# Another count of TensorE's instructions in a kernel's planner, and rows transposed through DRAM and VectorE in place of TensorE

## The chip, the cores and the metric

The kernel runs on one core of one Trainium2 chip. A core has five engines that run side by side, each with its own queue, in order: TensorE (PE; its weight loads are listed as PEld), VectorE (DVE), ScalarE (ACT), GpSimd (POOL) and SyncE (SP), which here issues nearly all DMAs. The metric is the device time in microseconds (us) of one execution. A profiled execution is a run of its own, with a time of its own.

## The reference

Two blocks follow one another, all in float32.

```python
# q, k, v: (4, 8, 768, 48) = batch, heads, steps, head size; beta: (4, 8, 768)
k_n = k / (np.linalg.norm(k, axis=-1, keepdims=True) + 1e-06)
for t in range(S):
    y[:, :, t] = np.einsum('bhd,bhde->bhe', q[:, :, t], state)
    v_old = np.einsum('bhde,bhd->bhe', state, kt)
    state = state + bt[:, :, :, None] * np.einsum('bhd,bhe->bhde', kt, vt - v_old)
x = y.transpose(0, 2, 1, 3).reshape(B * S, H * D)      # 3072 tokens of 384
rms = np.sqrt(np.mean(x * x, axis=-1, keepdims=True) + 1e-06)
xn = x / rms * rms_g
g = xn @ w_gate                                        # 384 x 1536
out = (g * (1.0 / (1.0 + np.exp(-g))) * (xn @ w_val)) @ w_out
```

The first is a recurrence over 768 steps (a delta rule), the second a gated feed-forward layer on its normalized output.

## The kernel before

**Tiling.** The steps are cut into 12 chunks (c = 0 to 11) of 64 steps. A chunk has 4 x 64 = 256 tokens, two tiles of 128. For each chunk there are these parts, each a function:

- `load`: k, q, v from DRAM by DMAs on SP; `norms` (L621): the inverse norms of k.
- `prep` (L812): k scaled and transposed on TensorE (`turn`, L582), scores of k with k (L605), a triangular inverse by 15 double steps on VectorE (L908, L914), for which the matrix is laid out anew through DRAM (dkk, dx, dxt), and a merge on TensorE (L963, L983). The merge uses half of the tile yn as scratch (L972).
- `qpart` (L638): q transposed and scores of q with k (L605). From chunk 2 on, q is brought into SBUF in squares of 32 x 32 by 16 small DMAs, and one VectorE transpose that works on 32 x 32 squares (`square_turn`, L613) does the rest.
- `recur` (L1000): products of k and q with the state (L1022), the inverse times the rest (L1069), and two products whose results are the chunk's output and the change of the state (L1105, L1174). The output rows are put into yn (128 x 2 x 384; L1044 and L1205), their mean square is taken (L1211), the root on GpSimd (L1224), and L1239 scales yn by it. Then yn has to be transposed into xf (128 features x 6 blocks of 128 columns), with the feature gains g_sb put in: six TensorE transposes into PSUM (L1256) and six ScalarE scalings out of it (L1260). Seven sums on VectorE (L1275) make the other eleven blocks of xf that the fast matrix product needs.
- `ffn` (L1403), chunks 2 to 11: 30 products, each four 128 x 128 x 128 matmuls (L1416), with evacuations on ScalarE (L1428) and VectorE (L1426), then the gate (L1432, L1433). `down` (L1454) does seven products of six matmuls each (L1473), with sums before and after (L1465, L1482), and stores. Chunks 0 and 1 go through `ffn_plain` (L1323, L1305).

yn and xf have one buffer each. xf of chunk c can be written only when the last product (L1416) of chunk c-1 has read it; yn is free again when it has been transposed.

**What sets the order.** Nothing is issued as the functions are called. Each call of `P.add` records an operation with its engine, a modelled duration, its dependencies, its PSUM banks and, for TensorE, `size`, its number of instructions (a float32 matmul counts four: two weight loads and two matmuls). `Plan.run` (L225) then makes many rounds: `forward` (L117) is a list scheduler that takes, over all engines, the operation that can start first (ties by a key), `backward` (L197) makes new keys from the latest starts, and these are shaken by random numbers. The round with the earliest modelled end gives the order, and in this order the operations are issued to their engines. The model has a penalty for a change of TensorE's tile shape (STICK) and an account of TensorE's instructions: a backlog that grows by `size` and falls at a fixed rate (FETCH, AHEAD; FETCH0, AHEAD0 before 130 us). A backlog over the store makes an operation's key worse by 2 x STICK, and its end later.

Until 70 us on the model's clock, TensorE is given filler matmuls (L1579) when it would stand idle.

Of the kernel before, what the change touches and what calls it, by code (L numbers as in the profile page):

```python
# [22 lines left out]
STRETCH = {"PE": 1.5, "ACT": 1.5, "DVE": 1.4, "POOL": 1.2, "SP": 1.0}  # L23
ENGINES = ("PE", "ACT", "DVE", "POOL", "SP")
OVERLAP = {"PE": 0.0, "ACT": 0.1, "DVE": 0.08, "POOL": 0.06, "SP": 0.0}
ROUNDS = 150
FETCH, AHEAD = 67.0, 160.0
EARLY, FETCH0, AHEAD0 = 130.0, 42.0, 130.0
STICK = 1.0
EARLYN = ()  # L30
RELEASE = (4.7, 29.5, 32.8, 35.2, 41.3, 40.8, 44)
KSQ, XSQ = 99, 99
DRAIN, REFILL, GRACE = 0.1, 0.2, 0.0
SHAKE = 0.12
SPARE = 1.0
# [22 lines left out]
def fillers(a, b):  # L58

    if a == 0.0:  # L60
        return [4, 4, 1]
    n, t = [], a
    while t < b - SPARE:
        n.append(4 if b - t > 1.5 else 2 if b - t > 0.9 else 1)
        t += 0.22 * n[-1] + 0.02
    return n


class Plan:
# [47 lines left out]
    def forward(self, banks, until):  # L117

        at = dict.fromkeys(ENGINES, 0.0)
        held = {"DVE": 0.0, "POOL": 0.0}  # L120
        cand = {e: [] for e in ENGINES}
        free = list(banks)
        for op in self.ops:
            op.wait, op.at = len(op.deps), op.ready
            for g in op.acquire:
                g.taken, g.uses = False, g.left
            if not op.wait:
                cand[op.eng].append(op)
        order, server, end_, mode = [], 0.0, 0.0, 0
        backlog = 0.0  # L130
        lanes = [0.0] * 8
        while len(order) < len(self.ops):
            best = None
            for e in ENGINES:
                for op in cand[e]:
                    s = max(op.at, at[e])
                    if op.dma:
                        s = max(s, lanes[0])
                    if op.port:
                        s = max(s, held["POOL" if e == "DVE" else "DVE"])  # L140
                    n = sum(not g.taken for g in op.acquire)
                    if n > len(free):
                        continue
                    if n:
                        s = max(s, free[n - 1])
                    key = op.key + (STICK if op.mode is not None and op.mode != mode else 0.0)
                    rate, store = (FETCH, AHEAD) if s > EARLY else (FETCH0, AHEAD0)
                    if op.size and backlog + op.size - rate * op.dur > store:
                        key += 2.0 * STICK
                    seen = max(at["PE"], s - GRACE) if op.mode is not None and op.mode == mode < 128 else s  # L150
                    if best is None or (seen, key, op.n) < best[0]:
                        best = (seen, key, op.n), op, s
            if best is None:
                return None
            _, op, s = best
            cand[op.eng].remove(op)
            for g in op.acquire:
                if not g.taken:
                    g.taken = True
                    free.pop(0)  # L160
            op.start = s
            if op.mode is not None and op.mode != mode:
                s += DRAIN if op.mode < 128 else REFILL
                op.start, mode = s, op.mode
            end = s + op.dur
            if op.eng == "PE":
                if s - at["PE"] > 1.4 and s > until:
                    end += 1.6
                rate, store = (FETCH, AHEAD) if s > EARLY else (FETCH0, AHEAD0)
                fill = 6.0 if s < until else 0.0  # L170
                backlog = max(0.0, backlog - (rate - fill) * (s - at["PE"])) + op.size - rate * op.dur
                late = max(0.0, backlog - store) / rate
                backlog, end = max(0.0, backlog - rate * late), end + late
            at[op.eng] = end - min(OVERLAP[op.eng], op.dur)
            if op.port:
                held[op.eng] = end
            end_ = max(end_, end)
            for g in op.release:
                g.uses -= 1
                if not g.uses:  # L180
                    free.append(end + 0.1)
                    free.sort()
            if op.dma:
                server = max(end + 0.9, server) + op.work
                end = server
                lanes = lanes[1:] + [end + 0.7]
            op.end = end
            for u in op.users:
                u.wait -= 1
                u.at = max(u.at, at[op.eng] if u.eng == op.eng and not op.dma else end + op.hop(u) + u.slack)  # L190
                if not u.wait:
                    cand[u.eng].append(u)
            order.append(op)
        self.end = end_
        return order
# [28 lines left out]

    def run(self, free, filler=None, until=0.0):  # L225
        self.first_priorities()
        best = None
        self.ends = []
        rng = random.Random(47)
        for k in range(ROUNDS):  # L230
            order = self.forward([t for t, _ in free], until if filler else 0.0)
            if order is None:
                break
            self.ends.append(self.end)
            if best is None or self.end < best[0]:
                best = self.end, [(op, op.start) for op in order]
            self.backward()
            for op in self.ops:
                if op.first:
                    op.key = op.n - 2000.0  # L240
                op.key += SHAKE * (k % 3) * rng.uniform(-1.0, 1.0)
        self.end = best[0]
        pe = 0.0
        free = list(free)
        for op, s in best[1]:
            op.start = s
            for g in op.acquire:
                if g.t is None:
                    g.t = free.pop(0)[1]
            if filler and op.eng == "PE":  # L250
                if s < until:
                    filler(fillers(pe, s))
                pe = s + op.dur
            op.fn()
            for g in op.release:
                g.left -= 1
                if not g.left:
                    free.append((s + op.dur + 0.1, g.t))
                    free.sort(key=lambda x: x[0])
# [1355 lines left out]
```

## Time and profile before

| what | us |
|---|---|
| median of 3 runs (698.35 to 700.17) | 698.62 |
| the profiled execution | 695.48 |
| its span, first to last instruction | 693.8 |
| PE: time in which a matmul ran | 679.1 (98%) |
| PEld: time in which weights were loaded | 619.7 (89%) |
| DVE busy | 540.1 (78%) |
| ACT busy | 304.0 (44%) |
| POOL busy | 139.9 (20%) |
| products L1416, both groups, x2400 | 181.6 + 124.6 |
| transposes of yn L1256, x72 | 10.9 |
| transposes of q on VectorE L613, x10 | 12.4 |

How to read the rows of the profile: a group is "line, engine, operation, out<-in, shape, xcount | busy us, mean ns of one | idle time of the engine before them and what ended it". A float32 matmul of the program stands as two rows of MATMUL and two of LDWEIGHTS. Matmuls are pipelined, so a mean of 277 ns is longer than the pitch at which they follow one another. "issue" means that an engine waited for nothing that the profile shows. A queue's name with a q at the end (SPq) is the engine's sequencer. In the list of DMAs the last number is the median time from issue to landing.

### The profile page before, as it was taken

What the parts mean: (1) busy time and instruction counts of PE and PEld (TensorE: products, weight loads), DVE (VectorE), ACT (ScalarE), POOL (GpSimd) and SP (SyncE); (2) the same over time, 40 slices, a digit from 0 to 9 for tenths busy, and PEclk for the clock granted to TensorE, in tenths of its full rate; (3) what the DMA queues carried; (4) which work ended last, traced back from release to release, by engine and by line L of the source; (5) the groups of instructions that cost most, each with busy time, mean ns of one, the idle gap of its engine ahead of it and who ended that gap; (6) DMA issues with size and microseconds to landing.
All of it is one profiled execution on the core that took longest, in us unless ns stands there. A gap on an engine that the chain in (4) does not pass through costs nothing.

```text
span 693.8 us, 23437 instructions
## 1 busy us (share of the span) xinstructions
PE 679.1 (98%) x10068; PEld 619.7 (89%) x10068; DVE 540.1 (78%) x1131; ACT 304.0 (44%) x735; POOL 139.9 (20%) x143
## 2 busy tenths in 40 slices
PE   7999999999999999999999999999999999999997
PEld 4577877778799999999999999999999999999997
DVE  4577899999899679599479589579779849966473
ACT  5265442424255346345345346255336346136240
POOL 6002041013213203404122133123032104000000
PEclk9999999999999999999999999999999999999999
DMA  8799973735611631532621542442353151130001
GB/s 158 151 228 213 272 186 95 136 57 88 104 26 27 114 55 29 105 61 44 107 46 25 90 69 38 88 62 46 64 80 53 27 90 34 24 55 2 24 1 24
DMA packets 236584, 55.47 MB, mean 80 GB/s; under 512 B 225856, under 2 KB 228928, under 8 KB 236480
## 3 DMA queue, kind: packets, MB, share of 16 engines
q1 hardware_dynamic: 232304, 53.19, 39.7%
q8 instruction: 79, 1.29, 0.8%
q10 hardware_dynamic: 4176, 0.79, 0.6%
q14 instruction: 25, 0.20, 0.1%
HBM read 40.83 MB, written 13.11 MB: 78 GB/s over the span
## 4 chain that ended last, share of the span: by engine, by line
PE 93%; DVE 2%; issue 1%; POOL 1%; DMA 1%; ACT 0%; SPq 0%; DVEq 0%; POOLq 0%; ACTq 0%
PE bank L1416 39%; PE bank L1473 20%; PE bank L1323 9%; PE bank L1305 4%; PE bank L605 4%; PE bank L1022 3%; PE bank L1579 2%; PE bank L1105 2%; PE bank L1069 2%; PE bank L582 2%; PE bank L1095 1%; PE bank L1256 1%; PE bank L1174 1%; PE bank L963 1%; POOL knrm L630 1%
## 5 line engine op out<-in xcount | busy, mean ns | idle before, releaser
L1416 PE MATMUL bank<-xf,w_in 128*128 128x128 f32 x1440 | 181.6, 277 | 0.1
L1426 DVE TENSOR_TENSOR tmp<-tmp,bank 128x512 f32<-128x512 f32 x180 | 121.1, 683 | 68.0 <-PE bank L1416 59.0
L1416 PEld LDWEIGHTS bank<-xf,w_in 128*128 128x128 f32 x1440 | 170.4, 192 | 2.8 <-issue 0.8
L1416 PE MATMUL bank<-xf,more 128*128 128x128 f32 x960 | 124.6, 277 | 1.5 <-DVE yn L1205 0.9
L1416 PEld LDWEIGHTS bank<-xf,more 128*128 128x128 f32 x960 | 115.2, 192 | 3.9 <-DVE yn L1205 1.0
L1428 ACT COPY tmp<-bank 128x512 f32<-128x512 f32 x120 | 68.9, 586 | 85.9 <-PE bank L1416 59.4
L1432 ACT ACTIVATE tmp<-tmp 128x256 f32<-128x256 f32 x120 | 49.8, 418 | 84.3 <-DVE tmp L1426 84.1
L914 DVE TENSOR_REDUCE acc<-acc 128x30 f32<-128x90 f32 (+4 forms) x150 | 71.0, 473 | 5.2
L630 POOL TENSOR_TENSOR knrm<-ksum,half 128x16 f32<-128x16 f32 x12 | 35.4, 2952 | 157.6 <-DVE ksum L629 156.0
L1473 PE MATMUL bank<-wo_sb,hf 128*128 128x192 f32 x360 | 63.6, 328 | 0.0
L1473 PEld LDWEIGHTS bank<-wo_sb,hf 128*128 128x128 f32 x360 | 58.1, 190 | 0.4
L1433 DVE TENSOR_TENSOR hf<-tmp 128x256 f32<-128x256 f32 x120 | 50.6, 439 | 7.5 <-ACT tmp L1432 7.0
L908 DVE TENSOR_TENSOR acc<-acc,at 128x60 f32<-128x60 f32 (+4 forms) x150 | 52.9, 353 | 1.6
L934 POOL COPY acc<-acc 128x128 f32<-128x128 f32 x40 | 20.9, 552 | 102.6 <-DVE acc L914 101.8
L861 POOL TENSOR_TENSOR at<-at,beta_b 128x1024 f32<-128x1024 f32 x8 | 19.3, 2407 | 104.6 <-DMA at<-dkk 88.4
L1305 PE MATMUL bank<-wo_sb,hf 128*128 128x384 f32 x96 | 34.7, 490 | 0.0
L1323 PE MATMUL bank<-xf,w_in 128*128 128x256 f32 x144 | 33.6, 383 | 0.0
L1323 PE MATMUL bank<-xp,w_in 128*128 128x256 f32 x144 | 33.5, 382 | 0.0
L1323 PEld LDWEIGHTS bank<-xf,w_in 128*128 128x128 f32 x144 | 26.9, 190 | 4.9 <-issue 0.2
L1482 DVE TENSOR_TENSOR tmp<-tmp,bank 128x192 f32<-128x192 f32 x30 | 10.5, 350 | 26.5 <-PE bank L1473 26.5
L1323 PEld LDWEIGHTS bank<-xp,w_in 128*128 128x128 f32 x144 | 26.8, 190 | 4.7
L1579 PE MATMUL bank<-ident 128*128 128x512 f32 (+2 forms) x60 | 27.2, 585 | 1.4 <-POOL ident masks.py:199 1.4
(185 smaller groups left out, 1030.6 us busy)
## 6 DMA issues: line engine op xcount, KB each, us to landing
at<-dkk SPq DMA_DIRECT2D x20, 256.0 KB, 3.8
more<-in_moe_w_gate_dram SPq DMA_DIRECT2D x6, 768.0 KB, 6.6
vt<-in_v_dram SPq DMA_DIRECT2D x24, 192.0 KB, 4.8
more<-in_moe_w_val_dram SPq DMA_DIRECT2D x6, 768.0 KB, 5.6
more<-in_moe_w_out_dram SPq DMA_DIRECT2D x6, 768.0 KB, 5.7
out_dram<-tmp SPq DMA_DIRECT2D x48, 96.0 KB, 2.2
k<-in_k_dram SPq DMA_DIRECT2D x23, 192.0 KB, 4.1
dkk<-kk SPq DMA_DIRECT2D x40, 64.0 KB, 1.9
```

The costliest lines, as they stand in the source:

```text
L630: P.add("POOL", 2.95, lambda: nc.gpsimd.tensor_tensor(out=knrm[i2], in0=ksum[i2], in1=half, op=ALU.pow), pn, r=[("ksum", i2), "half"], w=[ ...
L908: nc.vector.tensor_tensor(out=acc[:, 1:3, 0:n, j + 2 : W].rearrange("p a i t -> p i a t"), in0=acc[:, old, 0:n, j : j + 2, None].to_broadc ...
L914: nc.vector.tensor_reduce(out=acc[:, new, 0:n, j + 2 : W], in_=acc[:, lo : lo + 3, 0:n, j + 2 : W].rearrange("p a i t -> p i t a"), axis=A ...
L1305: nc.tensor.matmul(po[p].t[:, 0:DM], hf[:, spot(f), 128 * p : 128 * p + 128], wo_sb[:, spot(f)], start=(f == f0), stop=(f == f1 - 1), skip ...
L1323: nc.tensor.matmul(ps.t[:, TOK * side : TOK * side + TOK], w_in[:, side, h_, 3 * t + i_, n : n + 128], x_[:, 2 * t : 2 * t + 2].rearrange( ...
L1416: nc.tensor.matmul(g.t[:, 128 * z : 128 * z + 128], fac[:, side, 128 * f : 128 * f + 128], xf[:, xs], start=(begin and z == 0), stop=False ...
L1426: P.add("DVE", V(512), lambda t=t, g=g: nc.vector.tensor_tensor(out=t, in0=t, in1=g.t, op=ALU.add), -1, r=[g], w=[tk], last=g)
L1428: P.add("ACT", A(512), lambda t=t, g=g: nc.scalar.copy(t, g.t), -1, r=[g], w=[tk], last=g)
L1432: P.add("ACT", A(256), lambda t=t: nc.scalar.activation(out=t[:, 0:256], in_=t[:, 0:256], func=ACTF.Silu), -1, w=[tk])
L1433: P.add("DVE", V(256), lambda t=t, f0=f0, p=p: nc.vector.tensor_tensor(out=hf[:, spot(f0) : spot(f0) + 2, 128 * p : 128 * p + 128], in0=t[ ...
L1473: nc.tensor.matmul(g.t[:, 0:192], a_[:, f], b_[:, f], start=(begin and f == 0), stop=(f == 5), skip_group_check=True)
L1579: nc.tensor.matmul(warm[:, 0 : 128 * w_].rearrange("p (w n) -> p w n", n=128), ident, ident[:, None, :].to_broadcast([128, w_, 128]))
```

## The change

**The planner.** The backlog is replaced by a count of TensorE's instructions in blocks of 256. `supply` goes through an operation's instructions: at number 140 of a block the next block is asked for (2.4 us to react, at least 3.45 us after the asking before, and 2.6 us to land), and at number 193 of a block TensorE stands still if that block has not landed. The delay is added to the operation's end; in the choice it is added to the start that is compared, in place of the key's penalty. There are 300 rounds instead of 150, and the random numbers start from 1 instead of 47. All the rest of the order follows from this anew, from the first chunk on.

**The rows.** XSQ goes from 99 to 4, so that in chunks 4 to 11 `recur` takes a branch which stood in the kernel already and was not used:

```python
if c >= XSQ:
    for p in range(2):
        dma(dyn[p], yn[:, p], px, r=[("yn", p)], w=[("dyn", p)], work=0.6)
    for z in range(4):
        src = dyn.rearrange("p (tq t) (k z f) -> z t k (p tq) f", t=32, z=4, f=32)[z]
        dst = yn[32 * z : 32 * z + 32].rearrange("s p n -> s (p n)").rearrange("s (k m f) -> s k m f", k=KT, f=32)
        dma(dst, src, px, r=[("dyn", 0), ("dyn", 1)], w=[("yn", 0), ("yn", 1), ("ysq", z)], work=0.6)
    P.add("DVE", V(768), lambda: nc.vector.transpose(out=xf[:, 0:6]..., in_=yn...), px, r=[("yn", 0), ("yn", 1)], w=xkeys)
    for k_ in range(KT):
        P.add("ACT", A(256), lambda k_=k_: nc.scalar.mul(xf[:, 2 * k_ : 2 * k_ + 2], ..., g_sb[:, k_ : k_ + 1]), pxv, ...)
    continue
```

The scaled rows go to DRAM by two DMAs (L1242) and come back into yn by four (L1246), each 32 partitions of 32 x 32 squares; one VectorE transpose of 768 columns (L1247) turns all squares into xf, and three ScalarE scalings of 256 columns (L1249) put the gains in, in place. The six TensorE transposes (L1256) and six scalings (L1260) of these chunks are gone, with their PSUM banks. The seven sums stay.

The diff, cut to its core:

```diff
-ROUNDS = 150
-FETCH, AHEAD = 67.0, 160.0
-EARLY, FETCH0, AHEAD0 = 130.0, 42.0, 130.0
+ROUNDS, SEEDS = 300, (1,)
+BLOCK, ASKED, LACKED = 256, 140, 193
+REACT, TURN, LAND = 2.4, 3.45, 2.6
...
-KSQ, XSQ = 99, 99
+KSQ, XSQ = 99, 4
...
+        def supply(s, dur, n0, size, keep):
+            late, last, got = 0.0, asked, {}
+            for k in range(int(n0) // BLOCK, int(n0 + size) // BLOCK + 1):
+                for mark in (ASKED, LACKED):
+                    n = BLOCK * k + mark
+                    if not n0 < n <= n0 + size:
+                        continue
+                    t = s + late + dur * (n - n0) / size
+                    if mark == ASKED:
+                        last = max(t + REACT, last + TURN)
+                        got[k + 1] = last + LAND
+                    else:
+                        late += max(0.0, got.get(k, usable.get(k, 0.0)) - t)
+            if keep:
+                usable.update(got)
+            return late, last
...
-                    if op.size and backlog + op.size - rate * op.dur > store:
-                        key += 2.0 * STICK
-                    seen = max(at["PE"], s - GRACE) if op.mode is not None and op.mode == mode < 128 else s
+                    seen = s
+                    if op.size and s >= until:
+                        seen += supply(s, op.dur, count, op.size, False)[0]
...
-                backlog = max(0.0, backlog - (rate - fill) * (s - at["PE"])) + op.size - rate * op.dur
-                late = max(0.0, backlog - store) / rate
-                backlog, end = max(0.0, backlog - rate * late), end + late
+                if s < until:
+                    count += 4 * len(fillers(at["PE"], s))
+                if op.size:
+                    late, asked = supply(s, op.dur, count, op.size, True)
+                    count += op.size + (0.5 if op.size in (16, 128) else 0.0)
+                    end += late
+                    self.lag += late
...
-        rng = random.Random(47)
-        for k in range(ROUNDS):
+        for seed, k in itertools.product(SEEDS, range(ROUNDS)):
+            if not k:
+                rng = random.Random(seed)
+                for op, key in zip(self.ops, first):
+                    op.key = key
```

GRACE is 0, so the removed form of `seen` was the same as s.

More of the change, by code (lines that the diff above doesn't have):

```diff
@@ L129, in forward @@
         order, server, end_, mode = [], 0.0, 0.0, 0
-        backlog = 0.0
+        self.lag = 0.0
+        count, asked, usable = 0.0, -9.0, {}
+        def supply(s, dur, n0, size, keep):
[14 more added lines that the diff above has]
+            return late, last
         lanes = [0.0] * 8
@@ L146, in forward @@
                     key = op.key + (STICK if op.mode is not None and op.mode != mode else 0.0)
-                    rate, store = (FETCH, AHEAD) if s > EARLY else (FETCH0, AHEAD0)
-                    if op.size and backlog + op.size - rate * op.dur > store:
-                        key += 2.0 * STICK
-                    seen = max(at["PE"], s - GRACE) if op.mode is not None and op.mode == mode < 128 else s
+                    seen = s
+                    if op.size and s >= until:
+                        seen += supply(s, op.dur, count, op.size, False)[0]
                     if best is None or (seen, key, op.n) < best[0]:
@@ L168, in forward @@
                     end += 1.6
-                rate, store = (FETCH, AHEAD) if s > EARLY else (FETCH0, AHEAD0)
-                fill = 6.0 if s < until else 0.0
-                backlog = max(0.0, backlog - (rate - fill) * (s - at["PE"])) + op.size - rate * op.dur
-                late = max(0.0, backlog - store) / rate
-                backlog, end = max(0.0, backlog - rate * late), end + late
+                if s < until:
[5 more added lines that the diff above has]
+                    self.lag += late
             at[op.eng] = end - min(OVERLAP[op.eng], op.dur)
@@ L226, in run @@
         self.first_priorities()
+        first = [op.key for op in self.ops]
         best = None
         self.ends = []
-        rng = random.Random(47)
-        for k in range(ROUNDS):
+        for seed, k in itertools.product(SEEDS, range(ROUNDS)):
[3 more added lines that the diff above has]
+                    op.key = key
             order = self.forward([t for t, _ in free], until if filler else 0.0)
             if order is None:
-                break
+                continue
             self.ends.append(self.end)
```

## The prediction

> **What bounds the kernel now.** I read the page first (parts 1, 2, 4, 5, 6), then the busy time by stage, then the rows of the lines that the change touches, then the waits of TensorE, VectorE and the SP queue, and last the order of time around one chunk's hand-over. From the page:
>
> ```profile
> span 693.8 us, 23437 instructions
> PE 679.1 (98%) x10068; PEld 619.7 (89%) x10068; DVE 540.1 (78%) x1131; ACT 304.0 (44%) x735; POOL 139.9 (20%) x143
> ...
> q8 instruction: 79, 1.29, 0.8%
> ...
> PE 93%; DVE 2%; issue 1%; POOL 1%; DMA 1%; ACT 0%; SPq 0%; DVEq 0%; POOLq 0%; ACTq 0%
> ```
>
> 93% of the chain that ended last is TensorE, and no other engine has more than 2%. The line of q8 is instruction blocks: 1.29 MB in 79 packets is 16 KB each. TensorE issues some 20,368 instructions (10,184 weight loads are in the trace, each with its matmul; the page's count of matmuls misses some), and 20,368 / 256 is 79.6, so these are TensorE's blocks of 256. The stages say the same:
>
> ```profile
> 0.00:70.00 70.00, 63.19 (x1048) 43.47 (x1049) 43.71 (x113) 36.52 (x89) 17.60 (x23) 1.00 0.89 187
> 70.00:186.00 116.00, 115.27 (x1530) 90.81 (x1529) 111.05 (x210) 44.09 (x101) 18.74 (x17) 1.00 0.62 139
> 186.00:654.00 468.00, 465.18 (x7220) 450.18 (x7220) 365.29 (x772) 212.78 (x522) 103.60 (x104) 1.00 0.32 55
> 654.00:694.00 40.00, 35.50 (x280) 35.20 (x278) 20.09 (x37) 10.56 (x24) 0.00 (x0) 0.98 0.07 16
> ```
>
> The columns are stage, length, then busy time of PE, PEld, DVE, ACT, POOL, then granted clock, DMA share and GB/s. From 186 us on TensorE is full: 465.2 of 468 us, at full clock, with VectorE at 78%, ScalarE at 45%, DMA at 32%. What shortens TensorE's own work there shortens the kernel; what only keeps another engine busier doesn't, until TensorE must wait for it.
>
> **Part 1: the transposes of the normalized rows, chunks 4 to 11 (XSQ 99 to 4).** The rows concerned:
>
> ```profile
> L1256 PEld LDWEIGHTS bank<-ident,yn 128*128 128x128 f32 x72 | 8.4, 141 | 2.3 <-ACT yn L1239 1.4 <-issue 0.5
> L1260 ACT ACTIVATE xf<-bank,g_sb 128x128 f32<-128x128 f32 x66 | 18.7, 374 | 3.3 <-PE bank L1256 3.3
> L1432 ACT ACTIVATE tmp<-tmp 128x256 f32<-128x256 f32 x120 | 49.8, 418 | 84.3 <-DVE tmp L1426 84.1
> L613 DVE STREAM_TRANSPOSE qt<-q 128x1024 f32<-128x1024 f32 x10 | 12.4, 1238 | 0.8 <-PE bank L1416 0.7
> ```
>
> *TensorE loses* 6 transposes a chunk in 8 chunks, 48 of the 72. By the weight-load row all 72 cost 8.4 us, so 48 cost 8.4 x 48/72 = 5.6 us. They run among full-array products, so no change of tile shape goes with them. This is on the path: **-5.6 us**.
>
> *ScalarE* loses 48 scalings of 374 ns (18.0 us) and gains 24 on 256 columns, SBUF to SBUF; by the nearest row (L1432, 418 ns) that is 10.0 us. Net -8 us on an engine with half its time free: nothing.
>
> *VectorE* gains 8 transposes of 768 columns: 1238 ns x 768/1024 = 0.93 us each, 7.4 us together, hidden while VectorE has 468 - 365 = 103 us free from 186 on. If that cover were gone it would cost 7.4 us. It is there: the waits view puts 59.0 us of VectorE's idle time down to products (VectorE waits for TensorE, not the reverse).
>
> *The DMAs* are new: two stores of yn (196 KB each in rows of 1536 B) and four loads back (98 KB each in runs of 128 B), in SP's queue.
>
> ```profile
> vt<-in_v_dram SPq DMA_DIRECT2D x24, 192.0 KB, 4.8
> out_dram<-tmp SPq DMA_DIRECT2D x48, 96.0 KB, 2.2
> k<-in_k_dram SPq DMA_DIRECT2D x23, 192.0 KB, 4.1
> q<-in_q_dram SPq DMA_DIRECT2D x80, 32.0 KB, 2.6
> at<-dkk SPq DMA_DIRECT2D x20, 256.0 KB, 3.8
> ```
>
> The last number is us from issue to landing. Consecutive issues stand about 0.6 us apart (16 q loads took 9.53 us on SP from 320.89). Round trip = second store 0.6 later + store landing + three more load issues (1.8) + load landing. Low: 0.6 + 2.2 (out) + 1.8 + 2.6 (q) = 7.2 us. High: 0.6 + 3.8 (at) + 1.8 + 4.8 (vt) = 11.0 us. I take 0.6 + 2.2 + 1.8 + 4.1 (k, whose 1024 runs of 192 B are nearest to 768 of 128 B) = **8.7 us**. SP gets 6 x 0.6 = 3.6 us more to issue in a chunk of about 52 us. Traffic: 3072 runs of 128 B a chunk; q1 moved 232,304 packets in 39.7% of 16 engines' span, 19 ns each, so 3072 cost 58 us over 16 engines, 3.6 us, beside a DMA share of 0.32. It fits.
>
> *What the round trip delays.* Now, yn is ready (end of L1239) on average at the moment when the last product of the chunk before ends. Against that end it comes, chunks 4 to 11, at +1.2, -1.5, -0.2, +0.7, -3.5, +1.9, -0.2, +4.0 us, and the first product of the chunk follows 9.7, 9.7, 9.7, 10.1, 9.6, 14.7, 14.9, 10.4 us after it; in between TensorE does the down products of the chunk before and the recurrence. After the change the way from yn is 8.7 + 0.93 (transpose) + 3 x 0.42 (scaling) + 3.0 (the seven sums, 328.7 to 331.8 now) = 13.9 us. If nothing else moved, the first product would be late by yn's place + 13.9 - the gap: 5.4, 2.7, 4.0, 4.5, 0.8, 1.1, 0, 7.5, together 26.0 us. Two covers: the recurrence can be done earlier (in chunk 11 the last DMA that it needs, mt<-dx, is issued by 619.1 and lands 2.1 us later, by 621.2; the product that needs it, L1069, starts at 629.4: 8 us free), and when the first product starts now, 3, 3, 3, 3, 3, 2, 1, 2 down products of 1.95 us are still to do, which can be drawn ahead of it. With only the second cover, chunks 4 to 10 are hidden and chunk 11 keeps 7.5 - 3.9 = 3.6 us. With the high round trip the same sum leaves about 9 us, with both covers 0. The plan minimizes a modelled end in which such a delay counts, so both covers should be used; I take **+2.0 us**, about half of 3.6.
>
> A wait is added on VectorE: the transpose waits in order for four landings, and behind it stand evacuations of product banks. If it sits at its place 1 us too early, TensorE has banks for about one product (0.9 us) more. That is the rival below.
>
> Here a rule speaks against the change. The Trainium skill, "VectorE: DVE Perf Modes", section "Rules for kernel authors", says of a 128x128 transpose that TensorE should be used if a PSUM destination is acceptable. The rows agree that TensorE's is the shorter operation (0.70 us for six against 0.93 us and six DMAs); by the rule nothing would be won and the delay would stand.
>
> **Part 2: the plan (TensorE's instructions in blocks of 256, 300 rounds, another seed).** It issues the same work in another order everywhere. What the old count missed can be seen: TensorE stops where it waits for nothing shown, shortly after a q8 packet.
>
> ```profile
> 328.17 1.29 PE L605 MATMUL bank<-qt,kt 64*64 64x64 f32 x58
> 330.01 0.34 PE L605 MATMUL bank<-qt,kt 64*64 64x64 f32 x6 [0.55 <-issue]
> ```
>
> The packet began at 327.0 and took 1.49 us; TensorE goes on 1.5 us after its end, in the midst of one score. In the weight loads' record I find six such stops, each 1.4 to 1.65 us behind the end of a q8 packet: 0.91 us at 41.5, 1.37 at 65.9, 0.39 at 86.4, 0.69 at 329.2, 0.83 at 370.4, 1.04 at 473.4; 5.2 us together. Each follows two or three of the dense lines (L605, L1022, L1105, L1174; 128 instructions in about 1 us). The first three lie where the order is nearly forced. The new count foresees such a stop and picks another operation. Bounds: all gone, -5.2 us; as many or more made elsewhere, since the order is new, +2.6. I take half: **-2.6 us**.
>
> The Trainium skill, "Runtime: NRT & Kernel Launch", section "Instruction fetch mechanics", says that the cost of crossing such a 16 KiB boundary is mostly hidden. The trace agrees for 73 of 79 packets and differs for six; by the rule alone this term would be nothing.
>
> The other thing that an order sets is how often TensorE changes tile shape. From 186 to 654 I count 119 changes, which cost 24.9 us over the pitch of their instructions, 0.21 us each. The change keeps the penalty for them (STICK) and takes away another that drove dense operations apart. No row says which way the count goes; 12 changes either way are 2.5 us. I take 0.
>
> **Sum.** -5.6 + 2.0 - 2.6 = -6.2 us: the profiled execution (695.48 us, span 693.8) would become 689.3 us. The median of the three runs shown is 698.62 us, 3.1 above the profiled one; the difference carries over: 698.62 - 6.2 = **692.4 us**.
>
> **The rivals.**
>
> *Rows late (slower).* The six DMAs stand in SP's order behind something that waits, and yn is not made earlier, so the transpose holds VectorE, banks stay full and TensorE stops at each hand-over. For it: SP is in order and waited 99.1 us for the last sums before output stores, and 16 q loads (9.53 us) now sit right where the six must go:
>
> ```profile
> SPq L398 <- DVE tmp L1482: 99.1, 11, 33.3
> SPq L398 <- PE bank L1174: 73.0, 8, 15.1
> ```
>
> Against it: the covers above. Price: half of the 26.0 us uncovered, 13.0: 698.62 - 5.6 - 2.6 + 13.0 = 703.4 us. It decides the sign when over 8.2 us stay uncovered in eight chunks, about 1 us a chunk. The rule on transposes of the Trainium skill would have this outcome.
>
> *Given back (the same).* The transposes go, but the new order stops for instructions as often as the old (0 instead of -2.6), and waits and changes of shape eat the rest (+5 instead of +2.0): 698.62 - 5.6 + 5 = 698.0 us. For it: the order comes from a random search over a model, and no row bounds how well its times hold. This is also the case in which the plan doesn't do what its change says.
>
> *All of it (faster still).* Every stop for instructions gone, no delay, 12 fewer changes of shape: 698.62 - 5.6 - 5.2 - 2.5 = 685.3 us.
>
> **How the numbers follow.** Forecast (about 692.4; own range 688 to 696) 0.50, all of it 0.14, given back 0.16, rows late 0.20. About 0.3% (2.1 us) is what a measurement of this kernel can tell from no change. Faster: 0.50 + 0.14 = 0.64; the same 0.16; slower 0.20. The range must reach into both ends: 686 leaves out about a third of "all of it", 705 the upper part of "rows late" (an uncovered 26 us would be 716), about 0.1 each way or less.
>
> **What would show it.** Right: L1256 keeps 24 of 72 matmuls; a VectorE transpose of 768 columns (L1247) appears 8 times at about 0.93 us, with little idle time before it put down to DMA yn; yn ready (L1239) some 6 to 9 us earlier against the last product than now, or fewer down products left at the first product; TensorE's share of the chain as high as now; fewer stops behind q8 packets, 78 or 79 of them. Wrong: idle time of TensorE at L1416 put down to VectorE's sums or transpose at the hand-overs (rows late); stops behind q8 packets of 5 us or more, or well over 119 changes of shape (given back). The forecast as a whole falls if TensorE's stage from 186 us on isn't shorter by about the 5.6 us of its transposes.

## The result, and the profile after

The changed kernel takes 692.04 us (median of four runs, 689.72 to 694.22) against 699.39 us of the kernel before on the same chip: a ratio of 0.9897, 95% interval 0.9857 to 0.9937, or 7.2 us less. Forecast were 692.4 us and -6.2 us. The total came out; how it is made up did not, as the experiments show.

The profiled execution after is the slowest of its four (694.22 us, granted clock 0.993; the run of 689.72 us had 0.999), the profiled one before was faster than its runs around it. So the two spans differ by 1.3 us only, and these two profiles can't show where most of the 7.2 us comes from. First the page of the changed kernel, the lines that answer to those of before:

```profile
span 692.5 us, 23397 instructions
PE 673.5 (97%) x10014; PEld 615.0 (89%) x10014; DVE 545.8 (79%) x1139; ACT 302.5 (44%) x711; POOL 140.5 (20%) x143
...
q8 instruction: 78, 1.28, 0.8%
...
PE 83%; DVE 6%; DMA 5%; SPq 3%; issue 1%; ACT 1%; ACTq 0%; DVEq 0%
```

TensorE has 54 recorded matmuls fewer, one block of instructions fewer is loaded, and 83% instead of 93% of the last chain is TensorE: VectorE, DMAs and SP's queue now have 14% of it. (This share goes with the order more than with the rows: the versions below without the rows through DRAM have between 65% and 91%.) The stages (same columns as before):

```profile
0.00:70.00 70.00, 62.53 (x988) 43.50 (x989) 43.10 (x110) 36.79 (x89) 18.15 (x23) 1.00 0.88 191
70.00:186.00 116.00, 111.60 (x1451) 88.91 (x1451) 106.08 (x205) 41.95 (x96) 18.09 (x17) 0.97 0.60 127
186.00:654.00 468.00, 465.15 (x7312) 448.66 (x7311) 377.18 (x789) 213.18 (x503) 104.29 (x104) 1.00 0.39 71
654.00:694.00 40.00, 34.23 (x269) 33.93 (x267) 19.40 (x36) 10.54 (x24) 0.00 (x0) 0.95 0.06 14
```

From 186 us on, TensorE is as full as before, but puts 7,311 weight loads into the same 468 us instead of 7,220. From 70 to 186 us it lost 4 us and clock. The timeline shows where:

```profile
72.58 1.95 PE L1119 MATMUL bank<-u,wsum 64*64 64x48 f32 x58
78.92 0.66 PE L1119 MATMUL bank<-u,wsum 64*64 64x48 f32 x6 [4.40 <-issue]
```

The q8 packet that it waited for (it goes on 1.6 us behind its end) began at 75.9 us, 9.4 us after the packet before it, while weights were loaded (DMA share 0.85 from 74 to 80 us). TensorE stood for 4.4 us in the midst of one product, and from 75.9 to 82.7 us half the clock was granted. This early stop, ahead of all chunks whose rows go through DRAM, is the likely reason why this execution is the slowest of its four; the other three weren't profiled.

The rows of the new way (lines 24 further down than before), and its DMAs:

```profile
L1273 ACT ACTIVATE xf<-xf,g_sb 128x256 f32<-128x256 f32 x24 | 10.6, 498 | 15.4 <-DVE xf L1271 15.3
L1271 DVE STREAM_TRANSPOSE xf<-yn 128x768 f32<-128x768 f32 x8 | 7.8, 972 | 0.9 <-DMA yn<-dyn 0.5 <-DMA q<-in_q_dram 0.4
L1280 PEld LDWEIGHTS bank<-ident,yn 128*128 128x128 f32 x24 | 2.7, 141 | 1.8 <-ACT yn L1256 1.3 <-issue 0.2
```

```profile
dyn<-yn SPq DMA_DIRECT2D x16, 192.0 KB, 1.9
yn<-dyn SPq DMA_DIRECT2D x32, 96.0 KB, 2.9
```

The transposes left on TensorE are 24, at 2.7 us instead of 8.4. A VectorE transpose takes 0.97 us (0.93 expected), a scaling 0.50 us (0.42), a store lands after 1.9 us (2.2), a load after 2.9 us (4.1). VectorE waited 0.9 us in all before the eight transposes. In SP's queue, chunk 5:

```profile
319.32 0.85 SPq L422 DMA_DIRECT2D dyn<-yn  x2
321.78 2.00 SPq L422 DMA_DIRECT2D yn<-dyn  x3
328.15 0.33 SPq L422 DMA_DIRECT2D dxt<-acc  x1
329.12 2.87 SPq L422 DMA_DIRECT2D dkk<-kk  x4
332.04 0.49 SPq L422 DMA_DIRECT2D dxt<-acc  x1
332.57 0.58 SPq L422 DMA_DIRECT2D yn<-dyn  x1
```

The fourth load stands behind six other DMAs, some of which wait, so the round trip takes 16.2 us from the issue of the first store to the last landing. In the other chunks it takes 15.1 to 20.8 us, and 7.5 us in chunk 11, where 8.7 us (at most 11.0) were expected; the landings are as fast as expected, the place in the queue is what the estimate lacked. The plan can let it take so long, since yn was ready 11.7 us ahead of the last product that reads the old xf. Over chunks 4 to 11, yn is now ready 5.9 to 16.6 us ahead of that product (12 us on average; before, at the same moment), and 0 to 3 down products are left at the first product of the chunk (before 1 to 3).

### The profile page after: what moved, and what is told of

Read it like the earlier page. It is cut to its first block, busy times and chain, and to the rows that moved or that the text cites. A ratio compares the mean times of both kernels' runs of the same rounds, so it can differ in the third digit from the quotient of the medians.

```text
span 692.5 us, 23397 instructions
## 1 busy us (share of the span) xinstructions
PE 673.5 (97%) x10014; PEld 615.0 (89%) x10014; DVE 545.8 (79%) x1139; ACT 302.5 (44%) x711; POOL 140.5 (20%) x143
## 4 chain that ended last, share of the span: by engine, by line
PE 83%; DVE 6%; DMA 5%; SPq 3%; issue 1%; ACT 1%; ACTq 0%; DVEq 0%
PE bank L1440 35%; PE bank L1497 20%; PE bank L1347 9%; PE bank L1329 5%; PE bank L629 3%; PE bank L1046 3%; SPq L422 3%; PE bank L606 1%; PE bank L1129 1%; PE bank L1093 1%; PE bank L1119 1%; DMA out_dram<-tmp 1%; DMA at<-dfull 1%; DMA wsum<-dm 1%; DVE tmp L1450 1%
## 5 line engine op out<-in xcount | busy, mean ns | idle before, releaser
L1450 DVE TENSOR_TENSOR tmp<-tmp,bank 128x512 f32<-128x512 f32 x180 | 120.5, 680 | 41.4 <-PE bank L1440 35.6
L932 DVE TENSOR_TENSOR acc<-acc,at 128x60 f32<-128x60 f32 (+4 forms) x150 | 51.5, 344 | 12.4 <-POOL at L915 6.4
L1347 PE MATMUL bank<-xf,w_in 128*128 128x256 f32 x144 | 35.8, 399 | 0.0
L1347 PEld LDWEIGHTS bank<-xf,w_in 128*128 128x128 f32 x144 | 27.7, 198 | 5.4 <-ACT xf L1284 0.4
L1354 ACT ACTIVATE tmp<-bank 128x256 f32<-128x256 f32 x24 | 9.2, 382 | 48.0 <-PE bank L1347 46.7
L1506 DVE TENSOR_TENSOR tmp<-tmp,bank 128x192 f32<-128x192 f32 x30 | 10.5, 349 | 24.0 <-PE bank L1497 22.4
```

The lines of the kernel that those rows point to most:

```text
L932: nc.vector.tensor_tensor(out=acc[:, 1:3, 0:n, j + 2 : W].rearrange("p a i t -> p i a t"), in0=acc[:, old, 0:n, j : j + 2, None].to_broadc ...
L1347: nc.tensor.matmul(ps.t[:, TOK * side : TOK * side + TOK], w_in[:, side, h_, 3 * t + i_, n : n + 128], x_[:, 2 * t : 2 * t + 2].rearrange( ...
L1450: P.add("DVE", V(512), lambda t=t, g=g: nc.vector.tensor_tensor(out=t, in0=t, in1=g.t, op=ALU.add), -1, r=[g], w=[tk], last=g)
```

## The experiments

Ratios are against the kernel before on the same chip, whose medians there were 697.5 to 699.4 us; a ratio times 698 us is given as a difference. To compare TensorE's time I use one ledger for all profiles: each weight load is given the mean pitch that its kind has in the kernel before; what is over at a change of tile shape is the price of that change; what else is over is "rest" (stops and waits); fillers are apart.

| kernel | ratio (95%) | us | work | fillers | changes of shape, cost | rest | span |
|---|---|---|---|---|---|---|---|
| before | 1 | | 595.4 | 28.4 | 159, 30.7 | 33.0 | 693.8 |
| changed | 0.9897 (0.9857 to 0.9937) | -7.2 | 589.8 | 26.6 | 156, 31.7 | 38.2 | 692.5 |
| e1 plan only | 0.9937 (0.9919 to 0.9955) | -4.4 | 595.4 | 25.3 | 150, 31.3 | 32.0 | 690.2 |
| e2 rows only | 1.0026 (1.0001 to 1.0052) | +1.8 | 589.8 | 28.0 | 151, 31.2 | 40.6 | 695.8 |
| e3 seed 2 | 0.9846 (0.9827 to 0.9865) | -10.7 | 589.8 | 26.2 | 159, 33.2 | 30.1 | 685.5 |
| e7 plan only, seed 2 | 0.9902 (0.9877 to 0.9926) | -6.8 | 595.4 | 25.3 | 159, 31.4 | 31.2 | 689.5 |
| e12 seed 3 | 0.9884 (0.9850 to 0.9918) | -8.1 | 589.8 | 26.0 | 155, 32.4 | 34.9 | 689.3 |
| e13 plan only, seed 3 | 0.9876 (0.9841 to 0.9911) | -8.7 | 595.4 | 26.5 | 153, 30.9 | 31.8 | 690.8 |
| e5 transposes kept | 1.0025 (1.0005 to 1.0044) | +1.7 | 595.4 | 26.1 | 161, 32.5 | 36.3 | 696.6 |
| e6 same order without them | 0.9985 (0.9966 to 1.0005) | -1.0 | 589.8 | 26.1 | 161, 32.4 | 37.7 | 692.2 |
| e8 blocks shifted | 0.9954 (0.9931 to 0.9978) | -3.2 | 589.8 | 30.5 | 156, 31.1 | 41.4 | 699.0 |
| e9 second round trip | 1.0135 (1.0106 to 1.0164) | +9.4 | 589.8 | 27.3 | 174, 35.9 | 47.2 | 706.6 |
| e10 account alone | 0.9954 (0.9930 to 0.9977) | -3.2 | 595.4 | 26.9 | 160, 31.1 | 33.0 | 692.5 |
| e11 search alone | 0.9955 (0.9935 to 0.9974) | -3.1 | 595.4 | 27.7 | 159, 31.8 | 33.7 | 694.8 |

**The two parts apart.** e1 is the changed kernel with

```diff
-KSQ, XSQ = 99, 4
+KSQ, XSQ = 99, 99
```

> The changed kernel with XSQ back at 99: the new planner alone, rows transposed on TensorE as before. My theory (TensorE's own work bounds the kernel; the plan is worth -2.6 us, the rows -3.6 us net): about 699.4 - 2.6 = 696.8 us. Rival A (the whole gain is the new order, the rows are hidden anyway): about 692 us. Rival B (the plan gives nothing, the rows all): about 699.4 us.

Measured: 692.57 us. That looks like rival A, but the kernel before took 697.5 us on this chip, 1.9 less than beside the changed kernel; by ratio it is -4.4 us, between my number and A. So the plan is worth more than the -2.6 us that I took, and the rows with this start 2.8 us on top of it. e2 is the kernel before with

```diff
-KSQ, XSQ = 99, 99
+KSQ, XSQ = 99, 4
```

> The kernel before with XSQ = 4: the rows through DRAM under the old planner. My theory: 699.4 - 5.6 + 2.0 = 695.8 us, TensorE's idle time at the hand-overs small, yn ready some 6 to 12 us earlier than before. Rival A (all from the order): 699 us or more. Rival B: 692 us.

Measured: 697.94 us, +1.8 us: no gain. The rows themselves aren't late: yn is ready 10 to 16 us ahead of the last product. The ledger has TensorE's work 5.6 us lower, as it must (it counts the weight loads), and the rest 7.6 us higher. Part of the rest is stops for instructions. In this kernel's list of TensorE's work (start, us, line, count, idle time before):

```profile
360.88 0.89 PE L1174 MATMUL bank<-u,k 64*48 64x48 f32 x61
363.09 0.29 PE L1174 MATMUL bank<-u,k 64*48 64x48 f32 x3 [1.32 <-issue]
...
464.12 1.03 PE L1022 MATMUL bank<-state,qt 48*64 48x48 f32 x56
466.56 0.32 PE L1022 MATMUL bank<-state,qt 48*64 48x48 f32 x5 [1.41 <-issue]
```

Each comes 1.3 to 1.5 us behind the end of a q8 packet, three and five matmuls short of the end of a dense line. From the first product on such stops sum to 5.1 us here and 1.7 us in the kernel before; waits for VectorE and ScalarE, taken the same way, to 5.5 us against 2.6 us. (The stop of 1.04 us at 473.4 us, which the prediction counts among those for instructions, stands in the waits view as a wait for VectorE and is counted there.) The old account gave the new work an order with more of both.

**Three orders, with and without the rows.** Two parts whose sum isn't the whole call for more than one order. The search starts from a random number, so another start gives the same work in another order. e3 and e12 change

```diff
-ROUNDS, SEEDS = 300, (1,)
+ROUNDS, SEEDS = 300, (2,)
```

(e12: 3); e7 and e13 are the same with XSQ at 99.

> The changed kernel with the random numbers started from 2 instead of 1, so the same work in another order that the same search finds. My theory (the work removed is what counts, the order found matters little): 690 to 694 us. Rival (the result is luck of the order): over 3 us away from 692, in the range 686 to 700 us. If TensorE stops for instructions in the weight-loading stage, near 74 us, it is seen whether that goes with the order.

> The new planner alone (rows transposed on TensorE) with the random numbers of e3_seed2. If the rows are worth their TensorE work: 687.2 + 5.6 = 692.8 us, give or take the 3 us that two orders differ by. Rival (rows worth nothing under the new planner, as 692.6 against 692.0 with seed 1 looks): 687 to 688 us.

> The changed kernel with random numbers from 3. With e13_plan_only_seed3 it is a third pair for what the rows are worth under the new planner, after 0.9897 against 0.9937 (seed 1) and 0.9846 against 0.9902 (seed 2). Theory (rows worth most of their 5.6 us of TensorE work whatever the order): 686 to 693 us and 3 to 5.6 us below the other of the pair. Rival (the two pairs are luck): no difference, or the other sign.

> The new planner alone (rows on TensorE) with random numbers from 3. Theory: 690 to 696 us, 3 to 5.6 us above e12_seed3. Rival: no difference from it, or below it.

Measured: 687.21 us (e3), 691.24 (e7), 691.14 (e12), 689.89 (e13). The order does matter: e3 lies 4.8 us below the changed kernel with the same work by the medians, 3.6 us by the ratios (uncertain by some 3 us), outside of what I expected, and is the fastest version of the study, faster than both kernels. It has no such late block among the weights: its stop near 70 us is 0.9 us. With the rows against without, by ratios: -2.8 us (seed 1), -3.9 (seed 2), +0.6 (seed 3); on average -2.0 us, where TensorE's work falls by 5.6 in each. The third pair shows no gain, as its rival said; the intervals of two ratios leave each difference uncertain by 2 to 3 us, and the average by some 1.7 us. Part of what is given back can be seen in TensorE's waits from 186 to 690 us, seeds 2 and 3 without the rows and then with them (waits in all, times, longest). e7 and e3:

```profile
PEld bank L1440 <- DVE tmp L1450: 0.7, 3, 0.3
```

```profile
PEld bank L1440 <- DVE tmp L1450: 2.6, 2, 1.8
PEld bank L1440 <- DVE tmp L1506: 1.5, 1, 1.5
```

and e13 and e12:

```profile
PEld bank L1440 <- DVE tmp L1450: 0.8, 1, 0.8
```

```profile
PEld bank L1440 <- DVE tmp L1450: 4.8, 6, 1.7
```

L1450 and L1506 are VectorE's evacuations of PSUM banks. With the rows, TensorE waits 3.4 and 4.0 us more for a free bank; its stops put down to "issue" rise in the same stretch as well, from 3.2 to 5.8 us and from 3.7 to 7.3 us. VectorE's busy time in the whole kernel is 531.8 us in e7 and 551.7 us in e3: 7.8 us of the difference are the transposes, and 6.0 us are the same 70 sums of xf (L1299), which took 489 instead of 385 ns on average; why isn't shown. In the pair of seed 1 the wait for banks doesn't rise (4.2 us without the rows, 2.9 us with them), and there the changed kernel's loss is the early stop. So that the transposes cause these waits is likely in two orders and not shown.

**The same order, with and without the transposes.** e5 is the changed kernel with TensorE's transposes done as well, into a bank that is released at once:

```diff
+for p in range(2):
+    psx = Group()
+    def again(p=p, psx=psx):
+        for t in range(KT):
+            nc.tensor.transpose(psx.t[:, 128 * t : 128 * t + 128], yn[:, p, 128 * t : 128 * t + 128], ident)
+    P.add("PE", 0.34, again, px, r=[("yn", p)], w=[psx], ps=psx, last=psx, size=6)
```

> The changed kernel, in which TensorE does the six transposes of yn in chunks 4 to 11 as well, into a bank that nobody reads (xf is still made by the rows through DRAM). My theory: TensorE's 48 transposes cost their own 5.6 us, so about 692.0 + 5.6 = 697.6 us. Rival (the transposes were hidden in TensorE's idle time and the gain is from PSUM banks, ScalarE or the order): 692 to 693 us.

e6 keeps e5's planner and leaves `again` empty, so that all engines get the same order and TensorE 48 transposes fewer.

> The order of e5_transposes_kept to the last instruction, with its 48 extra TensorE transposes left out when the program is written (the planner still thinks that they are there, so nothing else moves). My theory: TensorE's work counts with its own length where the order is the same, so 699.5 - 5.6 = 693.9 us, a microsecond or two beside it, since the blocks of 256 shift by 96 instructions. Rival (freed time on TensorE is taken back by waits for evacuation): 698 us or more.

Measured: 699.49 us (e5) and 695.68 us (e6). e5 lies 7.5 us above the changed kernel by the medians and 8.9 us by the ratios, more than the 5.6 us of the transposes: it was planned anew and has another order. Between e5 and e6, with nothing else moved, lie 3.8 us by the medians (on two chips), 2.8 by the ratios (uncertain by 2 us) and 4.4 by the spans of the profiles (e6's is the fastest of its twelve): half of the 5.6 us or more, not all, and 1.8 us short of my number for e6. The 698 us of the rival did not come, but some of the freed time is taken back, as it said: rest rises by 1.4 us.

**The part in which the rows can act.** All eight chunks with the new rows lie behind the first product of chunk 2. Its place is seen in the list of one line's instructions (minimum, median and maximum in ns, then first and last start in us); before, changed, e7 and e3:

```profile
L1416 PEld LDWEIGHTS bank<-xf,more x960: 186/192/192, 185.5 to 674.6; 128*128 128x128 f32 x192
L1440 PEld LDWEIGHTS bank<-xf,more x960: 186/192/192, 184.5 to 673.3; 128*128 128x128 f32 x192
L1440 PEld LDWEIGHTS bank<-xf,more x960: 186/192/192, 182.7 to 670.3; 128*128 128x128 f32 x192
L1440 PEld LDWEIGHTS bank<-xf,more x960: 186/192/192, 177.6 to 666.4; 128*128 128x128 f32 x192
```

From there to the end of the span (us, rows on TensorE against rows through DRAM; the last column is how TensorE's work behind that place changes by the ledger, since a new order also moves work across it):

| pair | on TensorE | through DRAM | difference | of which TensorE's work |
|---|---|---|---|---|
| seed 1 (e1, changed) | 512.7 | 508.0 | -4.7 | -5.6 |
| seed 2 (e7, e3) | 506.8 | 507.9 | +1.1 | -4.9 |
| seed 3 (e13, e12) | 508.6 | 509.5 | +0.9 | -6.3 |
| old planner (before, e2) | 508.3 | 513.5 | +5.2 | -1.8 |
| same order (e5, e6) | 516.1 | 511.5 | -4.6 | -5.6 |

These are single executions. They show that with another order the whole gain can be given back behind that place: in seeds 2 and 3 waits and changes of shape there grow by 6 to 7 us. The 4 us that e3 is faster than e7 lie ahead of it, where no row goes through DRAM: e7 stood 2.1 us in the midst of a product at 51 us, with half the clock for 3.4 us after it. So the -2.0 us of the three pairs are not a measure of the rows alone.

**A second round trip.** e9 sends the squares to DRAM once more and back before the transpose:

```diff
+for z in range(4):
+    dma(dyn2[rows], yn[rows]..., px, r=[("yn", 0), ("yn", 1)], w=[("dyn2", z)], work=0.6)
+for z in range(4):
+    dma(yn[rows]..., dyn2[rows], px, r=[("dyn2", z_) for z_ in range(4)], w=[("yn", 0), ("yn", 1), ("ysq", z)], work=0.6)
```

> The changed kernel with a second round trip: the squares in yn go to DRAM once more and back, so that yn is 5 to 9 us later in xf, planned anew. My theory (the trip is hidden because the recurrence can be done earlier): 690 to 695 us, yn ready some 20 us ahead of the last product. Rival, rows late: 5 us or more slower than the changed kernel, with TensorE idle at the hand-overs or VectorE waiting for yn<-dyn2.

Measured: 707.40 us, 16.6 us above the changed kernel by ratio. My theory falls here, though yn is ready 22 to 33 us ahead of the last product, even more than the 20 us that it named. The chain of this kernel:

```profile
PE 48%; DVE 26%; issue 7%; SPq 7%; DMA 5%; POOL 5%; ACT 2%; DVEq 0%; POOLq 0%; ACTq 0%
```

and the two longest of TensorE's waits from 186 us on:

```profile
PEld bank L1447 <- ACT tmp L1459: 6.8, 6, 2.5
PEld bank L1447 <- DVE tmp L1457: 3.1, 9, 0.5
```

Under half of the chain is TensorE's work, though it is still busy for 458.9 of the 468 us from 186 to 654 us. It changes shape 174 times instead of 156 (4.2 us) and the rest is 9.0 us higher. Before its eight transposes VectorE now waits 7.4 us in all (3.5 of them put down to the rows' DMAs) instead of 0.9. The time is that of the rival "rows late"; its mechanism is seen in part only, since TensorE's longest waits are for ScalarE's evacuations, and what the longer trip does to the order isn't shown.

**What in the plan gains.** e10 is the kernel after with XSQ at 99, 150 rounds and the old start 47, so that only the account of instructions is new; e11 is the kernel before with 300 rounds and start 1.

> The kernel before with the new account of instructions alone: rows on TensorE, 150 rounds, random numbers from 47 as before. Theory (the plan's 4.4 us of e1_plan_only come from counting blocks, so that dense lines no longer run into the end of one): 691 to 695 us, stops behind an instruction packet of 5 us or less in all. Rival (they come from the longer search or another start): 697 to 699 us.

> The kernel before with its old account, but 300 rounds and random numbers from 1. Theory (blocks): 696 to 701 us, with stops behind instruction packets of 6 to 14 us as in before and e2_rows_only. Rival (search): 691 to 695 us.

Measured: 694.56 us (-3.2) and 695.40 us (-3.1). The account alone and the search alone come out alike: e10 as the theory of blocks said, e11 near what its rival, the search, said. But each is one order, e11 has another start as well as more rounds, and orders of the same work differ by more than these 3 us: what either gives by itself is not shown. Stops for instructions from the first product on are 0.3 us in e10, 0 to 0.6 in e1, e7 and e13, but 1.5 us in e11 and 1.7 before: there the new account does what it says. Over the whole profile the stops that end 1.2 to 1.8 us behind a packet sum to 2.4 us in e10 and 2.2 us in e11, against 5.2 us before. (A longer stop of 2.8 us in e10, at 66.5 us, ends 0.1 us after a DMA to wsum has landed, which the product behind it reads; it is a wait for data.)

e8 puts 128 instructions ahead of TensorE's work, in the changed kernel's own order:

```diff
+for _ in range(32):
+    nc.tensor.matmul(warm[0:32, 0:64], ident[:, 0:32], ident[:, 0:64])
```

> The changed kernel in its own order, with 32 small matmuls (128 instructions, half a block) put ahead of TensorE's first work, of which the planner knows nothing; they fall into the time before k lands. Theory (the plan gains because it counts where a block ends): the dense lines meet the ends of blocks again, stops for instructions of 3 to 7 us more, 695 to 699 us. Rival (the plan gains by a longer search, not by the count): 691 to 693 us.

Measured: 694.60 us, 4.0 above the changed kernel by ratio, and it settles nothing:

```profile
1.41 5.98 PE L1607 MATMUL bank<-ident 128*32 128x64 f32 x64 [1.41 <-POOL ident masks.py:199]
...
9.37 1.04 PE L606 MATMUL bank<-ident,k 128*128 128x128 f32 x8
```

The 64 recorded matmuls took 6.0 us, so that the first transpose of k starts at 9.4 instead of 5.8 us and the first chunk's work runs 2.5 to 3.1 us late. That, and not the blocks, can be the whole difference; its stops behind packets are no longer than the changed kernel's (2.0 us against 5.7). The profiled execution is also the slowest of its twelve (700.73 us).

## Why the prediction was right, and where not

**What bounds the kernel**: right that TensorE is full, from 186 to 654 us in all versions (458.9 to 467.8 of 468 us); but a full TensorE didn't mean that work taken off it shortens the kernel. The 5.6 us that are gone from the ledger are a count of weight loads at a fixed pitch, not a measured gain. (The 10,184 weight loads of the prediction take in 116 entries of the sequencer; the page has 10,068, and 20,136 / 256 = 78.7 gives the same 79 blocks.)

**The signs that it named.** L1256 kept 24 of 72, the VectorE transposes came out as said with 0.9 us of waiting, yn was early, and changes of shape from 186 to 654 us are 118 instead of 119. Three signs went the other way. TensorE's share of the chain fell. Stops behind packets did not get fewer in the profiled execution: 5.7 us against 5.2, 4.5 of them the early one (from the first product on 0.4 against 2.6); "5 us or more" was the sign of "given back". And the stage from 186 us on, on which the forecast as a whole was staked, isn't shorter: from the first product of chunk 2 to the end 508.0 us against 508.3. There the transposes took 5.6 us off, some 3 us of work came in that stood ahead of it before, and waits grew by some 2 us. By its own test the prediction's account of the gain fails for this execution, and that the total agreed is luck in good part.

**Rows, -5.6 + 2.0 = -3.6 us**: the first term is seen where the order is kept (e5, e6), the second looks mis-sized. Over three orders the rows are worth -2.0 us, so 3.6 us come back, where +2.0 was taken; with some 1.7 us of uncertainty this alone doesn't part from the forecast, but in the order of the old planner the rows gain nothing (+1.8 us), which does. It isn't the round trip, which took about twice the expected 8.7 us and was hidden all the same, as both covers said: yn comes 12 us earlier on average and VectorE waits 0.9 us for it. In two of three pairs it is in part TensorE's wait for VectorE's evacuations; I had put VectorE's added 7.4 us down as hidden in 103 us of idle time. An average of idle time didn't say that VectorE is free when a bank is due. Beside it stand stops put down to "issue" and the early part of each order.

The Trainium skill's rule to transpose on TensorE ("VectorE: DVE Perf Modes", "Rules for kernel authors") is neither borne out nor refuted here: -2.8, -3.9 and +0.6 us under the new planner, +1.8 us under the old.

**Plan, -2.6 us**: the step that failed is "all gone, -5.2 us" as the lower end, which counted only the stops for instructions. Measured over three orders the plan is worth -4.4, -6.8 and -8.7 us, -6.6 on average. The ledgers of e1, e7 and e13 against before show 2 to 3 us fewer fillers ahead of 70 us, and 1 to 2 us less rest; the first product of chunk 2 starts at 177.5 to 182.7 us instead of 185.5. That accounts for 3.0 to 4.3 us of span. The remaining 3.0 us on average (0.8 to 5.7) lie in good part in that the profiled execution of the kernel before (695.48 us) was faster than its medians (697.5 to 699.4), and no profile shows what its other executions lose. This stays open.

**The rivals.** "Rows late" did not happen with one trip; with two its time came, and its mechanism in part. "Given back" is half right: much of the rows' gain is given back, and the plan's larger gain hides it. That no row bounds what an order is worth was said and is the lesson: orders of the same work differed by 4.8 us (3.6 us by the ratios). So the total of -6.2 against -7.2 us is partly luck: by the three orders the rows were taken 1.6 us too good and the plan 4.0 us too poor, with the early stop of seed 1 on top.

## What to carry to other kernels

Work taken off a full engine can come back as waits for the engine that frees its buffers; look at the waits for banks, not at the average busy time of the other engine, and time the stage in which the work stood. A part whose effect is some tenths of a per cent in a kernel with a searched order has to be measured over several orders, with and without; here single pairs gave -3.9, +0.6 and, with the old plan, +1.8 us for the same edit. To price an operation by itself, keep the plan and leave it out at issue.

## What the runs showed of the hardware

A stop of TensorE can cost more than itself. Around the stop of 4.4 us the changed kernel was granted half the clock for 6.8 us, 3.8 us of them behind its end at 78.9 us:

```profile
74.00:80.00 6.00, 1.60 (x24) 1.39 (x20) 2.06 (x5) 0.00 (x0) 0.00 (x0) 0.66 0.85 118
80.00:90.00 10.00, 10.00 (x155) 8.53 (x155) 7.93 (x13) 2.27 (x5) 0.00 (x0) 0.86 0.84 230
```

(The column before the last two is the clock.) Stretches of 3.4 us at half the clock stand behind stops of 2.1 to 3.1 us in e1, e2, e7, e9 and e10, and of 1.6 us in e11, and one of 6.8 us behind a stop of 1.5 us in e13; other stops of 2.4 us in e5, 2.5 us in e9 and 2.8 us in e2 and e12 had none. The Trainium skill, "TensorE: Matmul & The Clock Gate", Part 1 on the clock gate, says that the gate goes by free-running windows of about 3.4 us; the stretches of 3.4, 6.8 and (e8, behind stops of 2.3 and 1.2 us) 10.2 us agree.

A stop for an instruction block can last much longer than the block's own packet: 4.4 us in the changed kernel, for a packet of 1.4 us, while weights were loaded. Whether those loads cause it wasn't tried; blocks 10.9 us apart, from 55.6 to 66.5 us, came without such a stop.
